# Attention block with cached keys: the second turn's keys transposed on TensorE, idle products at the start, other first loads, new orders

## The chip, the core and the metric

One core of a Trainium2 chip runs the whole program. Its engines are TensorE (PE: matmuls and transposes into PSUM), VectorE (DVE), ScalarE (ACT), GpSimd (POOL, here only the identity matrix) and SyncE (SP, here the queue that issues every load and store to the 16 DMA engines). The metric is the device time of one execution in microseconds; lower is better. Where runs are compared, it is the median.

## The reference

```
x: 8 x 112 x 640    k_cache, v_cache: 8 x 32 x 512 x 192    wq: 640 x 6144    wo: 6144 x 640   (bf16)
q      = (x @ wq) as 8 x 32 heads x 112 x 192
scores = einsum("bhqd,bhkd->bhqk", q, k_cache) * 192 ** -0.5
p      = softmax(scores)
o      = einsum("bhqk,bhkd->bhqd", p, v_cache)
out    = o as 8 x 112 x 6144 @ wo
```

## The kernel before, in words

**Turns and steps.** A turn t is one batch element with one half of the heads (16 heads): t = 0 to 15, batch t mod 8, half t div 8. A step n works on four heads: n = 0 to 63, turn n div 4. A unit u (0 to 15) is one head's keys or values within its turn, 512 rows of 192.

**Orders written out by hand.** Four texts at the top of the file (SP_WORK, PE_WORK, ACT_WORK, DVE_WORK) are lists of words, one list for each engine, and each engine works strictly in the order of its list. A word is a letter with numbers. Class Plan keeps for each operation what it depends on, and who must have read a buffer or a PSUM bank before it is overwritten (function `take` does this for the eight banks), and turns both into semaphore waits. An engine whose next word has to wait holds up all words behind it.

On SP: X loads token chunks of x (chunks of 128 tokens, 160 KB each), W loads a piece of wq for heads in pairs (W0.2.2: half 0, from pair 2, two pairs, 960 KB; one pair is 480 KB), U loads keys as they stand (untransposed) of the first turn into `kn`, K3 loads the keys of turn 3 transposed by the DMA engines into `kt[3 % 2]`, V10.8 loads the values of turn 10, units 8 to 15 (1536 KB), Y1.0 loads one half of wo's rows of head half 1 (1920 KB), Z stores. `kn` lies in the place of wo (`wo_flat`), and so does `vx`, the third home of values, used once by V1.0; Y0.0 and V1.0 therefore wait until the first turn's keys have been transposed. K of turn t waits for the last scores of turn t - 2, as there are two key buffers; a V waits until the products of the values that lay in its place are done.

On PE: X5.7 transposes token chunk 5 with bank 7; A0.3.6 and B0.3.4 compute the queries of head pair 3 for two batch elements (A: two 128-row blocks, ten matmuls of 224 columns; B: one, five matmuls); K6.0 transposes unit 6 of the first turn's keys, six 128 x 128 transposes; S5 computes the scores of step 5 into banks 0 to 3; T5.0.4 and T5.1.5 transpose its probabilities (eight transposes each) and V5.4 multiplies them with the values (16 + 16 matmuls); O are groups of four matmuls with wo, G and L the like of the last two turns, F the final transposes of the output.

On ACT and DVE: x, k, a, b, t, v copy the results of X, K, A, B, T, V out of PSUM (a and b are "q copies"); m is the scaling of the scores with the row minimum of the negated values, e the exponential with its row sum, r the reciprocal, n the normalisation, c two copies of queries into `qh` for step n (the "q copy" ahead of a step's scores), p, g, l the sums of O, G and L.

**Where the profile's lines are.** L399 X loads, L404 U loads, L411 W, L419 Y, L432 K, L445 V, L453 stores; L468 X, L477 K, L490 A and B, L521 to L538 scores, L548 T, L568 and L581 V, L597 O, L612 G, L627 L, L638 F; L650 all copies (function `copy`; the tile it writes tells which: kt, xT_sb, acc_q for queries, pT_sb, oT_sb), L675 and L676 c, L685 m, L695 e, L703 r, L710 n, L735 and L737 p.

**The start.** Before its first scores PE transposes x, fills queries, and transposes the first turn's keys, which come untransposed by U0.4, U4.8 and U8.16 (768, 768 and 1536 KB); all later turns' keys come transposed by DMA (K1 to K15). The two loads that are issued together in the profile at 23.79 are K1 and K2; K2 waits for the scores of step 3.

Q_PLACES gives each head pair's queries a place in `qp` for each pair of turns.

## Time and profile before

| | us |
|---|---|
| time, median of 3 runs (459.57 to 460.03) | 459.64 |
| the profiled execution's own time | 460.54 |
| its span, first to last instruction | 458.7 |
| PE busy | 438.4 |
| DVE busy | 360.8 |
| ACT busy | 347.3 |

The span is what the profile's times count in, from the first instruction; the execution's own time has some 1.8 us around it. A row of a view of instructions has start, duration, engine, line, operation, written tile <- read tiles, shapes, and in brackets the idle time of the engine before it and what ended it. A row of the chain of waits has start, share of the path, engine and line; matmuls there are counted from one end to the next, so many of them give the price of one in a dense row. A row of a view of windows has the stretch, its length, the busy time (and number of instructions) of PE, PEld, DVE, ACT and POOL, the granted PE clock, DMA's share and GB/s. A row of instruction groups has busy time, mean duration in ns, and idle time before.

### The profile page before, as it was taken

The numbers are of one execution on the slowest core, as the hardware profiler recorded it, in microseconds if no ns is written. First come the engines' busy times: TensorE is split into PE (matmuls) and PEld (weight loads), VectorE is DVE, ScalarE is ACT, GpSimd is POOL, SyncE is SP. The second block draws the span as 40 slices with busy tenths as digits, with TensorE's granted clock in tenths as the row PEclk, the third lists the DMA queues.
The fourth block names the chain that finished last, engine by engine and source line by source line (L and its number), as shares of the span: only waits on it lengthen the run. The fifth ranks groups of instructions, "written<-read, shape, count | busy, mean of one in ns | idle before, by whom it ended". The sixth has DMA issues, their size and how long they took to land.

```text
span 458.7 us, 14942 instructions
## 1 busy us (share of the span) xinstructions
PE 438.4 (96%) x6307; PEld 399.2 (87%) x6307; DVE 360.8 (79%) x1165; ACT 347.3 (76%) x787; POOL 0.7 (0%) x6
## 2 busy tenths in 40 slices
PE   4999899999999999999999999997999999999996
PEld 3889789888999888998989899997998999899996
DVE  0566768878889986789898888886868988979781
ACT  2577879867877878687886789766787788777683
POOL 0000000000000000000000000000000000000000
PEclk9899999999999999999999999999999999999999
DMA  8999999999989999999999999999999999996501
GB/s 278 372 350 224 241 327 352 237 306 287 260 215 247 362 275 214 308 243 331 206 337 209 309 235 326 300 189 368 225 274 260 281 287 261 219 253 222 178 14 51
DMA packets 234321, 119.63 MB, mean 261 GB/s; under 512 B 185744, under 2 KB 234256, under 8 KB 234256
## 3 DMA queue, kind: packets, MB, share of 16 engines
q1 hardware_dynamic: 234256, 118.69, 106.5%
q8 instruction: 49, 0.80, 0.7%
q14 instruction: 16, 0.13, 0.1%
HBM read 70.35 MB, written 1.15 MB: 156 GB/s over the span
## 4 chain that ended last, share of the span: by engine, by line
PE 87%; ACT 4%; DMA 4%; DVE 3%; issue 1%; SPq 0%; ACTq 0%
PE ps L490 18%; PE ps L597 17%; PE ps L581 12%; PE ps L548 10%; PE ps L536 7%; PE ps L568 7%; PE ps L521 6%; PE ps L523 6%; DMA wq_sb<-in_wq_dram 2%; ACT p_sb L695 2%; DMA vt<-in_v_cache_dram 2%; PE ps L612 1%; DVE s_sb L685 1%; PE ps L627 1%; ACT acc_q L650 1%
## 5 line engine op out<-in xcount | busy, mean ns | idle before, releaser
L695 ACT ACTIVATE p_sb<-s_sb,nmx 112x512 bf16<-112x512 f32 x256 | 183.1, 717 | 42.3 <-DVE s_sb L685 40.7
L685 DVE TENSOR_SCALAR_CACHE_REDUCE s_sb<-ps 112x512 f32<-112x512 f32 x256 | 172.9, 684 | 41.3 <-PE ps L538 16.9
L490 PE MATMUL ps<-xT_sb,wq_sb 128*128 128x224 bf16 x960 | 110.0, 262 | 2.7 <-DMA wq_sb<-in_wq_dram 0.9
L597 PE MATMUL ps<-oT_sb,wo_sb 128*128 128x224 bf16 x840 | 95.0, 259 | 0.8 <-ACT acc_q L650 0.4
L490 PEld LDWEIGHTS ps<-xT_sb,wq_sb 128*128 128x128 bf16 x960 | 88.6, 99 | 7.4 <-DMA wq_sb<-in_wq_dram 1.9
L710 DVE TENSOR_SCALAR p_sb<-p_sb,rinv 112x512 bf16<-112x512 bf16 x256 | 84.6, 349 | 3.2
L597 PEld LDWEIGHTS ps<-oT_sb,wo_sb 128*128 128x128 bf16 x840 | 77.1, 98 | 2.5 <-issue 0.7
L650 ACT ACTIVATE acc_q<-ps 128x224 bf16<-128x224 f32 (+1 forms) x128 | 55.9, 447 | 24.6 <-PE ps L490 19.8
L650 ACT ACTIVATE pT_sb<-ps 128x896 bf16<-128x896 bf16 x64 | 58.3, 911 | 13.0 <-PE ps L548 12.8
L548 PE MATMUL ps<-ident,p_sb 112*128 112x112 bf16 x1024 | 65.3, 213 | 0.1
L650 ACT ACTIVATE oT_sb<-ps 128x672 bf16<-128x672 f32 x64 | 46.5, 727 | 18.5 <-PE ps L581 16.2
L548 PEld LDWEIGHTS ps<-ident,p_sb 112*128 112x128 bf16 x1024 | 57.7, 98 | 2.5 <-DVE p_sb L710 0.7
L581 PE MATMUL ps<-pT_sb,vt 128*128 128x112 bf16 x992 | 59.5, 213 | 0.0
L581 PEld LDWEIGHTS ps<-pT_sb,vt 128*128 128x128 bf16 x992 | 49.8, 98 | 4.9
L695 ACT ACTIVATION_READ_ACCUMULATOR p_sb<-s_sb,nmx 112x1 f32 x256 | 49.2, 192 | 0.0
L650 DVE COPY pT_sb<-ps 128x896 bf16<-128x896 bf16 x64 | 39.7, 620 | 12.0 <-PE ps L548 11.2
L568 PEld LDWEIGHTS ps<-pT_sb,vt 128*64 128x64 bf16 x992 | 27.3, 109 | 16.8 <-ACT p_sb L695 7.2
L568 PE MATMUL ps<-pT_sb,vt 128*64 128x112 bf16 x992 | 36.2, 215 | 5.4 <-DVE p_sb L710 2.6
L521 PE MATMUL ps<-kt,acc_q 128*112 128x256 bf16 x128 | 35.2, 275 | 1.3 <-DVE kt L650 0.7
L523 PE MATMUL ps<-kt,acc_q 128*112 128x256 bf16 x128 | 34.9, 273 | 0.0
L521 PE MATMUL ps<-kt,qh 128*112 128x256 bf16 x128 | 34.9, 272 | 0.0
L523 PE MATMUL ps<-kt,qh 128*112 128x256 bf16 x128 | 34.9, 272 | 0.0
(50 smaller groups left out, 453.2 us busy)
## 6 DMA issues: line engine op xcount, KB each, us to landing
vt<-in_v_cache_dram SPq DMA_DIRECT2D x31, 1536.0 KB, 9.1
wo_sb<-in_wo_dram SPq DMA_DIRECT2D x4, 1920.0 KB, 13.5
wq_sb<-in_wq_dram SPq DMA_DIRECT2D x7, 960.0 KB, 10.7
wo_sb<-in_k_cache_dram SPq DMA_DIRECT2D x2, 768.0 KB, 9.1
wo_sb<-in_k_cache_dram SPq DMA_DIRECT2D x1, 1536.0 KB, 14.2
wo_sb<-in_v_cache_dram SPq DMA_DIRECT2D x1, 1536.0 KB, 7.8
out_dram<-xT_sb SPq DMA_DIRECT2D x8, 140.0 KB, 3.3
wq_sb<-in_wq_dram SPq DMA_DIRECT2D x2, 480.0 KB, 6.4
```

Source lines behind the costliest of these rows:

```text
L490: mm = e.matmul(ps[:, bank, j * S2:(j + 1) * S2], wq_sb[:, dc, c0:c0 + 128], xT_sb[:, dc, bp * S2:(bp + 1) * S2], start=(dc == 0), stop=(d ...
L521: e.matmul(ps[0:SQ, 2 * j, hs], ev, ktb[:, :, 0, cs(i)], start=(h == 0), stop=False, skip_group_check=True)
L523: mm = e.matmul(ps[0:SQ, 2 * j + 1, hs], od, ktb[:, :, 2, cs(i)], start=(h == 0), stop=False, skip_group_check=True)
L536: m1 = e.matmul(ps[0:SQ, 2 * j, hs], ev, ktb[0:64, :, 1, cs(i)], start=False, stop=True, skip_group_check=True)
L548: mm = e.transpose(psb[:, bank, c:c + SQ], p_sb[:, (4 * n + 2 * j + h) % 8, q * 128:(q + 1) * 128], ident[0:SQ, 0:SQ])
L568: mm = e.matmul(ps[64 * h:64 * h + 64, b0 + j, SQ:2 * SQ], vtb[:, h0 + 2 * j + h, d0:d0 + 64], pT(j, h, q), start=(q == 0), stop=(q == 3))
L581: mm = e.matmul(ps[:, b0 + j, 2 * h * SQ:(2 * h + 1) * SQ], vtb[:, h0 + 2 * j + h, d0:d0 + 128], pT(j, h, q), start=(q == 0), stop=(q == 3))
L597: mm = e.matmul(ps[:, bank, j * S2:(j + 1) * S2], wo_sb[:, KU * (u % 2) + k, m * 128:(m + 1) * 128], oT_sb[:, u % NO, k, :], start=(k == 0 ...
L650: return e.activation(dst, src, ACTF.Copy) if eng == "ACT" else e.tensor_copy(dst, src)
L685: return e.tensor_scalar(s_sb[:, a, :].rearrange("p (e c) -> p e c", e=2), ps[0:SQ, 2 * j:2 * j + 2, h * 256:(h + 1) * 256], -scale, None, ...
L695: return e.activation(p_sb[:, k, :], s_sb[:, a, :], ACTF.Exp, bias=nmx[:, k:k + 1], scale=-1.0, accum_out=rsum[:, k:k + 1])
L710: return e.tensor_scalar(p_sb[:, k, :], p_sb[:, k, :], rinv[:, k:k + 1], None, op0=ALU.mult)
```

## The change

Five things change together.

1. U words carry a turn: U1.0.8 and U1.8.16 load the second turn's keys untransposed into the same `kn`, after the first turn's unit in that place has been transposed (`load_kn`), and K1 leaves SP's list. PE's list has 16 more K words (K1.3.4: turn 1, unit 3, bank 4), ACT's and DVE's lists 8 more copies each, into `kt[1]`. The scores of turn 1 wait for these copies. K3, which overwrites `kt[1]`, and K2, which overwrites `kt[0]`, wait for the copies too; Y0.0 and V1.0 wait for both turns' transposes.
2. D words: products of the identity with itself into a bank that nobody reads (`idle_products`). PE's list begins with 8 and 20 of them.
3. The first loads stand in another order on SP: W0.1.1 ahead of the first keys, then U0.0.4 and U0.4.8 one behind the other. V0.8 stands behind U1.8.16.
4. Q_PLACES has other places, and the lists of all engines are in a new order throughout. They hold the same work apart from 1 and 2. On SP, Y1.0 moves ahead of K10, Y0.1 ahead of K3, and V4.0 behind K5.
5. A further word, P, and functions for it (probabilities transposed by DMA) are new in the code; SP's list holds no such word, so the list `by_dma` is empty and they do nothing.

```
 SP_WORK = """
-X0.0.2 W0.0.1 U0.4 W0.1.1 W0.2.2 X1.2.4 X2.4.7 U4.8 W0.6.2 W0.4.2 U8.16 V0.0 V0.8
-K1
-K2 V1.0 V1.8 Y0.0 V2.0
-K3 V2.8 Y0.1 V3.0
-K4 V3.8 V4.0
-K5 V4.8 W1.4.2 W1.2.2 V5.0 W1.0.2
-K6 V5.8 V6.0
-K7 V6.8 W1.6.2 V7.0
-K9 V8.8 V9.0
-K10 V9.8 Y1.0 V10.0
-K15 V14.8 V15.0 V15.8 Z1 Z2 Z0 Z5 Z3 Z4 Z6 Z7
+X0.0.2 W0.0.1 W0.1.1 U0.0.4 U0.4.8 W0.2.2 X1.2.4 W0.6.2 W0.4.2 U0.8.16 X2.4.7 V0.0 U1.0.8 U1.8.16 V0.8
+K2 V1.0 V1.8 Y0.0 V2.0 Y0.1
+K3 V2.8 V3.0
+K4 V3.8
+K5 V4.0 V4.8 W1.0.2 W1.4.2 W1.2.2 V5.0
+K6 V5.8 W1.6.2 V6.0
+K7 V6.8 V7.0
+K9 V8.8 V9.0 Y1.0
+K10 V9.8 V10.0
+K15 V14.8 V15.0 V15.8 Z0 Z5 Z1 Z4 Z3 Z2 Z6 Z7
...
 PE_WORK = """
-X1.4 X0.6 A0.0.6 B0.0.4 K0.6 B0.1.5 A0.1.7 K2.3 K3.0 K1.2 A0.3.6 X2.5
-S0 A0.2.7 K6.0 B0.3.4 K5.5 X4.0 X3.1 X5.7 B0.7.6 B0.2.5 K7.2 K4.0 B0.6.7
-S1 B1.2.7 B1.3.6 B1.6.7 A0.6.6 K11.0 K8.1 A0.7.7 T0.0.4 K12.1 B0.5.6 X6.0 A0.4.7 K9.0 K15.3 A0.5.6 K10.5 B0.4.7 K13.4
-A1.6.6 B1.0.7 T0.1.5
-S2 V0.4 K14.6 A1.1.7 A1.0.6 B1.7.7 T1.0.4 T1.1.5
-S3 V1.4 A3.0.7 T2.0.4 T2.1.5 B1.1.6 A1.4.7 B3.7.6
-S4 V2.4 B2.4.7
-S5 A2.4.6 B2.5.7 T3.0.4 A1.2.6 T3.1.5 A1.3.7
...
+D1.8.3 D0.20.3 X1.0 X0.4 A0.0.6 B0.1.5 A0.1.6 B0.0.4 K0.2.1 K0.0.0 K0.3.3 K0.1.2 K0.5.4 K0.4.5
+S0 B0.2.5 A0.3.7 A0.2.6 B0.3.5 K0.7.1 K0.6.4 A0.7.6 X3.5 B0.7.7
+S1 B0.6.6 B0.4.7 X2.4 A0.4.6 A0.5.7 K0.13.5 K0.12.0 K0.11.3 B0.5.7 K0.10.1 T0.0.4 K0.9.3 B1.0.6 X5.7 K0.14.0 K0.15.4
+K0.8.1 T0.1.5 A0.6.7
+S2 V0.4 A1.4.6 X6.1 B1.1.7 A1.1.6 T1.0.4
+S3 T1.1.5 K1.3.4 A3.0.7 K1.7.1 A1.6.6 V1.4 K1.4.0 K1.6.1 K1.1.2 K1.9.0 T2.0.4 K1.12.1 K1.5.6 K1.2.7 T2.1.5 X4.3
+K1.15.2 K1.0.1 A1.0.6 K1.14.7 K1.13.4
+S4 V2.4 K1.10.7 K1.8.0 A2.0.6 B1.7.7 K1.11.5 A3.5.6
+S5 B1.6.6 T3.0.4 B3.4.6 A1.3.7 T3.1.5 B1.4.6
...
 ACT_WORK = """
...
-e3.0 b1.1 e3.1 t2.0 e3.2 e3.3
-e4.0 a1.4 b3.7 e4.1 e4.2 v2 b2.4 e4.3 a2.4
...
+e3.0 k1.3 e3.1 k1.7 a3.0 a1.6 v1 e3.2 k1.1 k1.5 t2.0 k1.9 k1.15 e3.3 k1.13 a1.0
+e4.0 e4.1 v2 a2.0 b1.7 e4.2 k1.11 a3.5 e4.3 b1.6
...
 DVE_WORK = """
...
-m3.0 c4 c5 r2.1 n2.2 n2.3 m3.1 t2.1 m3.2 m3.3 r3.0
-m4.0 n3.0 m4.1 n3.1 m4.2 m4.3 r3.1 n3.2 n3.3 r4.0 n4.0
...
+m3.0 m3.1 t1.1 m3.2 m3.3 r2.1 n2.2 c4 k1.4 k1.6 n2.3 k1.12 k1.2 t2.1 k1.0 x4 r3.0 n3.0 n3.1 k1.14 r3.1
+m4.0 m4.1 c5 n3.2 k1.10 n3.3 m4.2 k1.8 m4.3 r4.0 c6 n4.0
...
 
         v_units = [(t, lo) for t in range(NT) for lo in (0, 8)]
         v_home = [0, 1, 2] + [(i + 1) % 2 for i in range(3, len(v_units))]
-        x_piece, wq_piece, kn_piece = {}, {}, {}
+        x_piece, wq_piece, kn_piece, by_dma = {}, {}, {}, []
         for kind, *a in work["SP"]:
+            if kind == "P":
+                by_dma.append(a[0])
             if kind == "X":
                 x_piece.update({c: ("X", a[0]) for c in range(a[1], a[2])})
             elif kind == "W":
                 wq_piece.update({(a[0], a[1] + i): ("WQ", *a) for i in range(a[2])})
             elif kind == "U":
-                kn_piece.update({u: ("KN", *a) for u in range(*a)})
+                kn_piece.update({(a[0], u): ("KN", *a) for u in range(a[1], a[2])})
+        kn_turns = sorted({t for t, _ in kn_piece})
 
         def q_both(m, lp):
             return [("Qa", m, lp), ("Qb", m, lp)]
...
                 return e.dma_start(xn[c0 // 4][:, c0 % 4:c0 % 4 + c1 - c0, :], src.rearrange("(c p) d -> p c d", p=128))
             add("SP", ("X", j), [], emit, f"mX{j}", 16)
 
-        def load_kn(lo, hi):
-            def emit(e):
-                return e.dma_start(kn[:, lo:hi, :], k_cache[0, lo:hi].rearrange("u (r q) d -> r u (q d)", q=4))
-            add("SP", ("KN", lo, hi), [], emit, f"mKN{lo}", 16)
+        def load_kn(t, lo, hi):
+            def emit(e):
+                return e.dma_start(kn[:, lo:hi, :], k_cache[t, lo:hi].rearrange("u (r q) d -> r u (q d)", q=4))
+            old = [("KT", t - 1, u) for u in range(lo, hi)] if t else []
+            add("SP", ("KN", t, lo, hi), old, emit, f"mKN{t}_{lo}", 16)
 
         def load_wq(half, lp, n):
             def emit(e):
...
             if half:
                 old = [d for w in range(u, NM, 2) for d in o_parts(w)]
             else:
-                old = [("KT", i) for i in range(HU)] + ([("PVm", 4, 1), ("PVm", 5, 1)] if u else [])
+                old = [("KT", *i) for i in kn_piece] + ([("PVm", 4, 1), ("PVm", 5, 1)] if u else [])
             add("SP", ("WO", half, u), old, emit, f"mWO{u}", 16)
 
         def load_k(t):
...
                 src = k_cache[b, half * HU:(half + 1) * HU].rearrange("u (r q) d -> (u r) (q d)", q=4)
                 return e.dma_start_transpose(kt[t % 2][:].rearrange("p a m c -> p (a m) c"), src)
             old = [("St", step_of(t - 2, s), 3) for s in range(4)] if t > 1 else []
+            old += [("evK", t - 2, u) for u in range(HU)] if t - 2 in kn_turns else []
             add("SP", ("K", t), old, emit, f"mK{t % 2}", 16)
 
         def v_tile(i):
...
                 return e.dma_start(v_tile(i)[:], src)
             old = [j for j in range(i) if v_home[j] == v_home[i]][-1:]
             old = [("PVm", step_of(v_units[j][0], v_units[j][1] // 4 + s), 1) for j in old for s in range(2)]
-            old += [("KT", u) for u in range(HU)] if v_home[i] == 2 else []
+            old += [("KT", *i) for i in kn_piece] if v_home[i] == 2 else []
             add("SP", ("V", t, lo), old, emit, f"mV{v_home[i]}", 16)
 
         def store(b):
             def emit(e):
                 return e.dma_start(out[b], xT_sb[0:SQ, b % DC, 0:D])
             add("SP", ("OUT", b), [("oout", b)], emit, f"mOUT{b % DC}", 16)
+
...
 
         holder = {}
...
             add("PE", ("XT", c), [x_piece[c]], emit)
             take(("XT", c), bank, ("XT", c), [("evX", c)])
 
-        def k_transposes(u, bank):
+        def k_transposes(t, u, bank):
             def emit(e):
                 for c in range(6):
                     mm = e.transpose(psb[:, bank, c * 128:(c + 1) * 128], kn[:, u, c * 128:(c + 1) * 128], ident[:, :])
                 return mm
-            add("PE", ("KT", u), [kn_piece[u]], emit)
-            take(("KT", u), bank, ("KT", u), [("evK", u)])
+            add("PE", ("KT", t, u), [kn_piece[t, u]], emit)
+            take(("KT", t, u), bank, ("KT", t, u), [("evK", t, u)])
+
+        def idle_products(i, n, bank):
+            def emit(e):
+                for _ in range(n):
+                    mm = e.matmul(ps[:, bank, 0:128], ident[:, :], ident[:, :], start=True, stop=True)
+                return mm
+            add("PE", ("D", i), [], emit)
+            take(("D", i), bank, ("D", i), [])
 
         def q_fill(part, m, lp, bank):
             half, bp = divmod(m, B // 2)
...
                         mm = e.matmul(ps[0:SQ, 2 * j + 1, hs], od, ktb[:, :, 2, cs(i)], start=(h == 0), stop=False,
                                       skip_group_check=True)
                     return mm
-                add("PE", ("Sm", n, j), [("qc", n)] + ([("evK", 4 * s + i) for i in range(4)] if t == 0 else [("K", t)]),
+                add("PE", ("Sm", n, j), [("qc", n)] + ([("evK", t, 4 * s + i) for i in range(4)] if t in kn_turns else [("K", t)]),
                     emit)
                 for b in (2 * j, 2 * j + 1):
                     take(("Sm", n, j), b, ("Sm", n, j), [("smax", n, 2 * j), ("smax", n, 2 * j + 1)])
...
             copy(eng, ("evX", c), [("XT", c)], xT_sb[:, :, c * 128:(c + 1) * 128],
                  psb[:, bank_of["XT", c], 0:D].rearrange("p (c s) -> p c s", c=DC))
 
-        def ev_k(eng, u):
-            copy(eng, ("evK", u), [("KT", u)], kt[0][:].rearrange("p a m c -> p (a m) c")[:, :, u * 128:(u + 1) * 128],
-                 psb[:, bank_of["KT", u], 0:768].rearrange("p (c r) -> p c r", c=6))
+        def ev_k(eng, t, u):
+            copy(eng, ("evK", t, u), [("KT", t, u)], kt[t][:].rearrange("p a m c -> p (a m) c")[:, :, u * 128:(u + 1) * 128],
+                 psb[:, bank_of["KT", t, u], 0:768].rearrange("p (c r) -> p c r", c=6))
 
         def ev_q(eng, part, m, lp):
             blocks = (0, 1) if part == "a" else (2,)
...
             def emit(e):
                 return e.activation(p_sb[:, k, :], s_sb[:, a, :], ACTF.Exp, bias=nmx[:, k:k + 1], scale=-1.0,
                                     accum_out=rsum[:, k:k + 1])
-            add(eng, ("exp", n, i), [("smax", n, i)] + ([("PT", n - 2, i // 2)] if n > 1 else []), emit)
+            old = [] if n < 2 else [("P", n - 2)] if n - 2 in by_dma else [("PT", n - 2, i // 2)]
+            add(eng, ("exp", n, i), [("smax", n, i)] + old, emit)
 
         def rc(eng, n, j):
             k = (4 * n + 2 * j) % 8
...
                  xT_sb[0:SQ, b % DC, 0:D], psb[0:SQ, bank_of["OF", b], 0:D])
 
         bank_of = {(k + "T", *a[:-1]): a[-1] for k, *a in work["PE"] if k in "XK"}
-        loads = {"X": load_x, "W": load_wq, "U": load_kn, "V": load_v, "K": load_k, "Y": load_wo, "Z": store}
+        loads = {"X": load_x, "W": load_wq, "U": load_kn, "V": load_v, "K": load_k, "Y": load_wo, "Z": store,
+                 "P": p_transposes}
         for kind, *a in work["SP"]:
             loads[kind](*a)
-        on_pe = {"X": x_transposes, "K": k_transposes, "A": lambda *a: q_fill("a", *a), "B": lambda *a: q_fill("b", *a),
+        on_pe = {"D": idle_products, "X": x_transposes, "K": k_transposes, "A": lambda *a: q_fill("a", *a), "B": lambda *a: q_fill("b", *a),
                  "S": scores, "T": transposes, "V": values, "O": o_sums, "G": o_six, "L": o_last, "F": o_final}
         for kind, *a in work["PE"]:
             on_pe[kind](*a)
```

The rows of the lists that are left out, and Q_PLACES, are changed in order only.

More of the change, by code (lines that the diff above doesn't have):

```diff
@@ L160 @@
[L160 to L172 removed]
+x1 a0.0 b0.1 b0.0 a0.1 k0.1 k0.5
@@ L454, in store, with p_spare, p_transposes @@
             add("SP", ("OUT", b), [("oout", b)], emit, f"mOUT{b % DC}", 16)
+        def p_spare(n):
+            return wq_flat[:, by_dma.index(n) * 16 * SQ:(by_dma.index(n) + 1) * 16 * SQ].rearrange("p (c s) -> p c s", c=16)
+        def p_transposes(n):
+            k = 4 * n % 8
+            def emit(e):
+                return e.dma_start_transpose(p_spare(n), p_sb[:, k:k + 4, :].rearrange("p a c -> p (a c)"))
+            old = [d for m in range(NM // 2, NM) for lp in range(LP) for d in q_both(m, lp)]
+            add("SP", ("P", n), [("norm", n, i) for i in range(4)] + old, emit, f"mP{n % 2}", 16)
         holder = {}
@@ L713, in ev_pt @@
         def ev_pt(eng, n, j):
-            copy(eng, ("evPT", n, j), [("PT", n, j)] + ([("PVm", n - 1, j)] if n else []),
+            old = [("PVm", w, j) for w in range(n) if w not in by_dma][-1:]
+            copy(eng, ("evPT", n, j), [("PT", n, j)] + old,
                  pT_sb[:, j, :, :].rearrange("p h c -> p (h c)"), psb[:, bank_of["PT", n, j], 0:8 * SQ])
```

378 lines of the change are left out of this document (190 added, 188 removed), and 16 rows, old and new, of the table Q_PLACES.

## The prediction

> **What bounds the kernel now.** The page first: the share of each engine.
>
> ```profile
> span 458.7 us, 14942 instructions
> PE 438.4 (96%) x6307; PEld 399.2 (87%) x6307; DVE 360.8 (79%) x1165; ACT 347.3 (76%) x787; POOL 0.7 (0%) x6
> ```
>
> PE is the bound: it is busy for 438.4 of 458.7 us. So time can be won in two ways only: less work on PE, or less waiting of PE. The view of windows, cut at the first scores (16.35) and at the second turn's first scores (51.73), says where it waits.
>
> ```profile
> 0.00:16.35 16.35, 9.82 (x79) 8.36 (x80) 2.79 (x7) 4.80 (x8) 0.70 (x6) 0.90 0.91 305
> 16.35:51.73 35.38, 33.74 (x438) 30.38 (x436) 24.08 (x72) 26.70 (x62) 0.00 (x0) 1.00 1.18 287
> 51.73:454.80 403.07, 394.70 (x5795) 360.49 (x5793) 333.97 (x1087) 314.88 (x717) 0.00 (x0) 1.00 1.08 258
> ```
>
> Of the 20.3 us that PE is idle, 6.5 lie before the first scores, 1.6 between them and turn 1, 8.4 in the long rest, and 3.9 after PE's end, where the last window is cut. The share before the last figure of a row is DMA's: it is about 1 everywhere, so loads are a second, near bound.
>
> PE's timeline and the chain of waits give the start, and the price of each kind of work.
>
> ```profile
> 4.03 1.23 PE L468 MATMUL ps<-ident,oT_sb 128*128 128x128 bf16 x10 [4.03 <-DMA oT_sb<-in_x_dram]
> ...
> 9.60 0.51 PE L477 MATMUL ps<-ident,wo_sb 128*128 128x128 bf16 x6 [0.96 <-DMA wo_sb<-in_k_cache_dram]
> 11.02 2.36 PE L490 MATMUL ps<-xT_sb,wq_sb 128*128 128x224 bf16 x15 [0.91 <-DMA wq_sb<-in_wq_dram]
> ...
> 16.35 0.27 PE L521 MATMUL ps<-kt,acc_q 128*112 128x256 bf16 x1
> ...
> 17.89 1.13 PE L490 MATMUL ps<-xT_sb,wq_sb 128*128 128x224 bf16 x10
> ```
>
> ```profile
> 13.38 1.90 PE ps L477 x18
> ...
> 30.16 0.96 PE ps L490 x10
> ...
> 33.83 0.67 PE ps L477 x12
> ...
> 39.89 0.51 PE ps L568 x16
> 40.41 0.89 PE ps L581 x16
> ...
> 44.03 0.79 PE ps L548 x16
> ...
> 51.73 0.11 PE ps L521
> ```
>
> Until 11 us PE's long waits end with loads. Prices, from these rows: an A fill of ten matmuls (L490) 0.96, a B of five 0.48, a K group of six transposes 0.34 (0.67/2), an X group of five 0.28, one step's scores 1.54 (16.35 to 17.89), a T group 0.40, a V group 1.40 (0.51 + 0.89).
>
> **The added PE work.** Turn 1's 16 units cost 96 transposes at 0.056 us (0.67/12): **+5.4 us**, all on the bounding engine. The 28 idle products stand ahead of the first data. At the unwarmed price of a 128-column product (1.90/18 = 0.106) they take 3.0 us; PE waits until 4.03 today, and they end near 4.6 if they start at 1.6 (an estimate: POOL writes the identity first, with six instructions of 0.7 us in all). The half microsecond is hidden, since the next thing after them that counts is a load at 11 us. Without that cover it would cost 0.5.
>
> What the products do to PE's clock is judged by these windows, whose third figure from the right is the granted clock.
>
> ```profile
> 4.90:8.30 3.40, 2.77 (x18) 2.02 (x16) 0.49 (x1) 0.92 (x2) 0.00 (x0) 1.00 0.99 321
> 8.30:11.70 3.40, 1.53 (x17) 1.11 (x15) 0.56 (x1) 0.55 (x2) 0.00 (x0) 1.00 1.06 382
> 11.80:15.10 3.30, 3.30 (x28) 2.98 (x27) 1.00 (x3) 0.81 (x2) 0.00 (x0) 0.50 1.07 370
> ```
>
> A stretch busy for 1.53 of 3.40 us was followed by one at clock 0.50; a stretch busy for 2.77 was not. The products should raise the clock early, but that wins nothing while loads set the pace, and the gaps that follow can lose it again; I count zero, with +1.7 (half of 3.4 us at half speed) as the upper end. The Trainium skill, page TensorE: Matmul & The Clock Gate, Part 4: PE-mode transpose, states that transposes do not count as busy for this clock. By that rule the added transposes would tend to the unwarmed price, 96 x 0.106 = 10.2 us. The trace disagrees: the last stretch above ends in 18 transposes, and 12 transposes at 33.83 ran at 0.056.
>
> **The first loads.** Landing times come from the DMA issues and their time to landing (10.5 us belongs to the issue at 7.51, 14.2 to that at 13.23).
>
> ```profile
> 7.51 1.76 SPq L404 DMA_DIRECT2D wo_sb<-in_k_cache_dram  x1
> ...
> 13.23 2.20 SPq L404 DMA_DIRECT2D wo_sb<-in_k_cache_dram  x1
> ...
> 23.79 35.28 SPq L432 DMA_TRANSPOSE kt<-in_k_cache_dram  x2
> ```
>
> ```profile
> DMA to landing us min/median/max: 10.5/10.5/10.5
> ```
>
> ```profile
> wo_sb<-in_k_cache_dram SPq DMA_DIRECT2D x1, 1536.0 KB, 14.2
> ```
>
> Units 4 to 7 landed at 18.0 and 8 to 15 at 27.4; between them came 960 + 960 + 1536 KB, so 368 KB/us. The first four pieces (320, 480, 768, 480 KB) are the same four in another order, so all of them are in by 11.0 again. The new list then has units 4 to 7 next: 11.0 + 768/368 = 13.1 us, and two K groups of them stand ahead of step 0's scores: 13.8. The chain on DVE is longer: three of its copies of K groups and the two halves of the q copy come between the last transposes and the scores.
>
> ```profile
> L650 ACT ACTIVATE kt<-ps 128x768 bf16<-128x768 bf16 x7 | 5.7, 811 | 2.0 <-PE ps L477 2.0
> L650 DVE COPY kt<-ps 128x768 bf16<-128x768 bf16 x9 | 5.0, 553 | 11.3 <-PE ps L477 11.2
> L675 DVE COPY qh<-acc_q 64x672 bf16<-64x672 bf16 x7 | 2.3, 329 | 0.9 <-ACT acc_q L650 0.6
> ```
>
> The third of four K groups ends near 12.1 (11.0 + 3 x 0.34), and the first copy starts: 12.1 + 3 x 0.55 + 2 x 0.33 = 14.4, so scores at 14.5 instead of 16.35. The new list has 0.6 less work ahead of them (one X and one A fewer, two K more: -0.28 - 0.96 + 0.67), so the wait recovered is 1.9 - 0.6 = **-1.3 us** (bounds 0, if the clock or a load is late, and -2.3).
>
> **From the first scores to turn 1.** The old list holds 4 X, 10 A, 13 B, 12 K, 4 scores, 6 T and 2 V here: 32.4 us by the prices, and 35.4 passed, so 3.0 were lost. In the new list the weights follow at 368 KB/us from 13.1 on: W0.2.2 at 15.7, W0.6.2 at 19.2, W0.4.2 at 21.8, units 8 to 15 at 26.0, and by the prices their users come at 16.0, 19.6, 23.3 and 26.0. So PE should run nearly without waits: I take **-2.2**, bounds -3.0 and 0. Turn 1's copies lie here too.
>
> ```profile
> L695 ACT ACTIVATE p_sb<-s_sb,nmx 112x512 bf16<-112x512 f32 x256 | 183.1, 717 | 42.3 <-DVE s_sb L685 40.7
> L650 ACT ACTIVATE pT_sb<-ps 128x896 bf16<-128x896 bf16 x64 | 58.3, 911 | 13.0 <-PE ps L548 12.8
> L650 ACT ACTIVATE oT_sb<-ps 128x672 bf16<-128x672 f32 x64 | 46.5, 727 | 18.5 <-PE ps L581 16.2
> ```
>
> ```profile
> L650 ACT ACTIVATE acc_q<-ps 128x448 bf16<-128x448 f32 x14 | 7.4, 539 | 4.9 <-PE ps L490 4.9
> ```
>
> Between the scores of steps 3 and 4 ACT's new list has 4 exps, 7 K copies, 3 q copies, one V and one T copy: 2.87 + 5.68 + 1.62 + 0.73 + 0.91 = 11.8 us. PE's has one step of scores, 13 K, 3 A, 3 T, one V and one X: 1.5 + 4.4 + 2.9 + 1.2 + 1.4 + 0.3 = 11.7. That is the tightest spot; the other nine copies go to DVE and to the steps around it.
>
> New waits on SP: the second key loads wait for turn 0's transposes (the last, K0.8, at about 30), and V0.8, K2 and all later loads queue behind them. V0.8's user is V2.4, behind step 4's scores at 50; after 26.0 come 480 KB and four pieces of 1536 KB, so V0.8 lands near 44. V1.0 and Y0.0 now wait for K1.11, behind step 4's scores, at some 54; before, SP sat in the issue of K1 and K2 until 59.1 (23.79 + 35.28). So neither costs time. The transposing load that goes frees DMA, and here nobody waits for it.
>
> **The long rest.** Two places lose much.
>
> ```profile
> 50.00:60.00 10.00, 8.85 (x111) 7.40 (x109) 7.86 (x27) 8.29 (x21) 0.00 (x0) 1.00 1.24 282
> ```
>
> ```profile
> 312.16 0.62 DVE L650 COPY pT_sb<-ps 128x896 bf16<-128x896 bf16 x1
> 313.43 0.27 PE L538 MATMUL ps<-kt,acc_q 64*112 64x256 bf16 x1
> 316.30 0.58 PE L568 MATMUL ps<-pT_sb,vt 128*64 128x112 bf16 x16 [2.60 <-DVE p_sb L710]
> ```
>
> ```profile
> 277.35 0.58 SPq L419 DMA_DIRECT2D wo_sb<-in_wo_dram  x1
> 282.75 24.27 SPq L432 DMA_TRANSPOSE kt<-in_k_cache_dram  x1
> 307.07 0.58 SPq L445 DMA_DIRECT2D vt<-in_v_cache_dram  x1
> ```
>
> ```profile
> DMA to landing us min/median/max: 9.1/9.1/9.1
> ```
>
> At 313 PE waits for V10.8, whatever the row names: its copies were done at 312.8, and V10.8, issued at 307.07 behind K11, landed 9.1 later, at 316.2. Ahead of K11 stood Y1.0 (277.35), 1920 KB or 5.2 us. The new list issues Y1.0 one turn earlier, ahead of K10, so K11 and V10.8 come sooner and K10 and V9.8 later: **-2.0** (bounds -2.7, and 0 where the wait only moves). The 1.15 us at 50 to 60 follow ten q copies in ACT's rows of steps 4 and 5; the new rows hold nine and a K copy: **-0.5** (0 to -1.15). The rest, some 4 to 5 us of PE's idling, is small waits that the new orders deal anew. Work between a step's scores and its first T group is at least 8.5 us in the new list (last step apart), in the old 7.6, 8.2 and 8.3 at three steps, and the end has one more L group between V63 and the last sums: **-1.0**, bounds +2.5 and -2.5.
>
> **Sum.** +5.4 - 1.3 - 2.2 - 2.0 - 0.5 - 1.0 = **-1.6 us**: span 457.1 for 458.7. The profiled execution took 460.54 in all, 1.84 around its span and 0.9 over the median of the runs, 459.64; the change against that median gives **458.0 us**, 0.35% faster.
>
> **Rivals.** (1) *The copies bind, slower.* ACT's 11.8 us beside 11.7 of PE between scores 3 and 4 hold up PSUM banks, and the terms -2.2, -0.5 and -1.0 go: 5.4 - 1.3 - 2.0 = +2.1, **461.7**. It decides once PE waits there for over 2 us on ACT or DVE copies of keys. For: the sums; against: DVE was busy for 24.1 and ACT for 26.7 of 35.4 us before. (2) *The V wait only moves* to K10 or V9.8 behind Y1.0: the -2.0 goes, **460.0**, and a new wait of a microsecond makes it 461. For: DMA is at 1 all along. (3) *The clock falls again* in the gaps near 12 to 14.5: +1.7, **459.7**. The Trainium skill, same page, Part 1: The HAM clock gate, has one idle window of about 3.4 us as the condition; the trace shows the fall after a window that was 45% busy. (4) *The new orders remove most small waits*: -2.2, -2.0 and -1.0 reach their lower bounds of -3.0, -2.7 and -2.5, another -3.0, **455.0**. For: 8.4 us are there to win. Against: every order leaves some.
>
> **Chances.** Forecast 0.34, rival 1 0.24, 2 0.14, 3 0.08, 4 0.20. Within 0.2% (0.9 us, what a measurement of this kernel can tell) lie 0.05 of the forecast, 0.07 of rival 2 and 0.03 of 3: 0.15. Faster is the rest of the forecast and rival 4: 0.49; slower rival 1 and the rests of 2 and 3: 0.36. The forecast's own range is 456.5 to 459; the range for all is 453.5 to 463.0: rival 1 with the clock's 1.7 (463.4) and rival 4 with -2.3 at the start and -1.15 at 50 to 60 (453.4) lie at its ends.
>
> **What would show it.** First scores near 14.5 and turn 1's near 50; no wait of over 1 us at V10.8; a K group at 0.34 us for turn 1. Wrong if first scores stay near 16, if PE waits on key copies in steps 3 to 5, or if a K or V load after Y1.0 is late.

## The result, and the profile after

The changed kernel takes **452.41 us** (median of 4 runs, 451.3 to 453.81) beside 459.61 for the kernel before (4 runs, 457.88 to 460.03): ratio 0.9852, 95% interval 0.9814 to 0.989. The profiled execution took 452.13 us with a span of 450.2. The forecast was 458.0, its range 453.5 to 463.0: the direction was right, the size far too small, and the time lies outside the range.

The first lines of the page of after:

```profile
span 450.2 us, 15210 instructions
...
PE 441.7 (98%) x6431; PEld 405.9 (90%) x6431; DVE 364.0 (81%) x1173; ACT 350.1 (78%) x795; POOL 0.7 (0%) x6
```

PE is busy 3.3 us longer than before (438.4) and the span is 8.5 us shorter, so PE's idle time fell from 20.3 to 8.5 us. Where it fell is read from the view of windows of after, cut again at the first scores (14.48) and at turn 1's first scores (49.90); the columns are window, length, and the busy time of PE, PEld, DVE, ACT and POOL, then granted clock, DMA share and GB/s.

```profile
0.00:14.48 14.48, 10.18 (x104) 8.94 (x104) 2.75 (x8) 5.49 (x9) 0.70 (x6) 1.00 0.87 297
14.48:49.90 35.42, 35.17 (x489) 32.96 (x490) 26.88 (x79) 30.00 (x67) 0.00 (x0) 1.00 1.12 328
49.90:446.90 397.00, 396.39 (x5841) 364.02 (x5838) 334.39 (x1088) 313.90 (x721) 0.00 (x0) 1.00 1.08 261
```

Idle of PE: 4.3 us before the first scores (6.5 before the change), 0.3 from there to turn 1 (1.6), and **0.6 in the long rest, where it was 8.4**. The view of waits of after, for PE, names nearly all that is left; its columns are the waiting line, what it waited for, microseconds in total, times, the longest.

```profile
PE ps L504 <- POOL ident L861: 1.5, 1, 1.5
PE ps L517 <- DMA wq_sb<-in_wq_dram: 1.0, 1, 1.0
PE ps L517 <- DVE xT_sb L678: 0.6, 1, 0.6
PE ps L496 <- DMA wo_sb<-in_k_cache_dram: 0.6, 1, 0.6
PE ps L548 <- DVE qh L704: 0.5, 1, 0.5
PE ps L666 <- DVE acc_q L793: 0.2, 1, 0.2
PE ps L517 <- ACT acc_q L678: 0.2, 1, 0.2
```

The first five lie ahead of the first scores. Behind them two waits of 0.2 us are left in 435 us. Neither the 2.6 us at V10.8 nor any wait of a V, T or O word on a copy is in the list.

The time from turn 1's first scores to the end is 458.73 - 51.57 = 407.16 before and 450.20 - 49.90 = 400.30 after. The new list holds 3.4 us more work there (three K groups, 1.0, and five B fills, 2.4, that stood ahead of step 4 before). So it takes 6.9 us less for 3.4 us more work: by the prices, 10.3 us less are lost. The view of windows shows 7.8 of it as idle, and 0.6 lies behind PE's end (3.9 us before, 3.3 after); the other 1.9 lie in stretches that it counts as busy. The forecast had 3.5 for these 10.3 (9.5 in the means of three profiles each, in the table below). That difference of 6.8 us is nearly the whole miss (the span fell by 8.5, forecast 1.6), and the experiments ask where it comes from: from the written orders, or from the loads, which the direct load of turn 1's keys relieves.

### The profile page after: what moved, and what is told of

It is laid out like the page before. It is cut to its first block, busy times and chain, and to the rows that moved or that the text cites. A ratio compares the mean times of both kernels' runs of the same rounds, so it can differ in the third digit from the quotient of the medians.

```text
span 450.2 us, 15210 instructions
## 1 busy us (share of the span) xinstructions
PE 441.7 (98%) x6431; PEld 405.9 (90%) x6431; DVE 364.0 (81%) x1173; ACT 350.1 (78%) x795; POOL 0.7 (0%) x6
## 4 chain that ended last, share of the span: by engine, by line
PE 95%; DMA 2%; ACT 2%; DVE 1%; issue 0%; SPq 0%
PE ps L517 20%; PE ps L625 18%; PE ps L609 13%; PE ps L575 11%; PE ps L563 8%; PE ps L595 7%; PE ps L548 6%; PE ps L550 6%; PE ps L496 2%; DMA wq_sb<-in_wq_dram 2%; PE ps L655 1%; PE ps L640 1%; PE ps L666 0%; ACT acc_q L678 0%; DVE kt L678 0%; ACT oT_sb L678 0%
## 5 line engine op out<-in xcount | busy, mean ns | idle before, releaser
L723 ACT ACTIVATE p_sb<-s_sb,nmx 112x512 bf16<-112x512 f32 x256 | 183.1, 718 | 35.2 <-DVE s_sb L713 33.8
L517 PE MATMUL ps<-xT_sb,wq_sb 128*128 128x224 bf16 x960 | 107.3, 260 | 1.9 <-DMA wq_sb<-in_wq_dram 1.0
L625 PE MATMUL ps<-oT_sb,wo_sb 128*128 128x224 bf16 x840 | 93.3, 259 | 0.0
L678 ACT ACTIVATE pT_sb<-ps 128x896 bf16<-128x896 bf16 x64 | 58.4, 913 | 15.9 <-PE ps L575 13.9
L678 ACT ACTIVATE oT_sb<-ps 128x672 bf16<-128x672 f32 x64 | 46.4, 726 | 22.6 <-PE ps L609 20.3
L548 PE MATMUL ps<-kt,acc_q 128*112 128x256 bf16 x128 | 35.2, 275 | 0.5 <-DVE qh L704 0.5
```

The costliest lines, as they stand in the source:

```text
L517: mm = e.matmul(ps[:, bank, j * S2:(j + 1) * S2], wq_sb[:, dc, c0:c0 + 128], xT_sb[:, dc, bp * S2:(bp + 1) * S2], start=(dc == 0), stop=(d ...
L548: e.matmul(ps[0:SQ, 2 * j, hs], ev, ktb[:, :, 0, cs(i)], start=(h == 0), stop=False, skip_group_check=True)
L625: mm = e.matmul(ps[:, bank, j * S2:(j + 1) * S2], wo_sb[:, KU * (u % 2) + k, m * 128:(m + 1) * 128], oT_sb[:, u % NO, k, :], start=(k == 0 ...
L678: return e.activation(dst, src, ACTF.Copy) if eng == "ACT" else e.tensor_copy(dst, src)
L723: return e.activation(p_sb[:, k, :], s_sb[:, a, :], ACTF.Exp, bias=nmx[:, k:k + 1], scale=-1.0, accum_out=rsum[:, k:k + 1])
```

## The experiments

For comparison across kernels, the text uses the stretch from 50 to 440 us, where every kernel here does plain steady work, and PE's idle time in it: 390 us less PE's busy time in the view of windows.

**1. No idle products.**

```diff
-D1.8.3 D0.20.3 X1.0 X0.4 A0.0.6 ...
+X1.0 X0.4 A0.0.6 ...
```

> The changed kernel without the 28 idle products. As the prediction had it (loads set the pace until 13 us, products worth nothing): first scores at 14.5, span within 0.5 us of the changed kernel's 450.2. Rival, the clock: without the products PE starts slow, a stretch near 8 to 15 us falls to clock 0.50, and the first scores or the fills behind them come 1 to 2 us later, with the end of the span as much later.

Measured: 453.28 us (10 runs), ratio to before 0.9905, interval 0.9869 to 0.9941; span 451.8, first scores at 15.50. The interval overlaps that of after. PE's waits in its view:

```profile
PE ps L487 <- DMA oT_sb<-in_x_dram: 3.9, 1, 3.9
PE ps L548 <- DVE qh L704: 1.3, 1, 1.3
```

The 1.5 us that PE waits in after before the products, and the products themselves, become a wait of 3.9 for the first tokens. The idle time from 50 to 440 is 1.0 us, so the clean rest doesn't hang on the products. The span is 1.6 us longer, where the expectation allowed 0.5, and the start shows why: the twenty query matmuls that follow W0.1.1 took nearly twice as long as in after. PE's timeline, without the products and with them:

```profile
8.39 3.83 PE L517 MATMUL ps<-xT_sb,wq_sb 128*128 128x224 bf16 x20 [0.59 <-DMA wq_sb<-in_wq_dram]
```

```profile
8.93 2.09 PE L517 MATMUL ps<-xT_sb,wq_sb 128*128 128x224 bf16 x20 [1.05 <-DMA wq_sb<-in_wq_dram]
```

So W0.1.1 came 0.5 us earlier, and the first scores 1.0 us later. The rival's slow start did come, though the granted clock of the windows reads 1.00 all along. What the products are worth in time isn't settled: the medians differ by 0.9 us, and the intervals overlap.

**2. Turn 1's keys by the transposing load, all else as changed.**

```diff
-... W0.4.2 U0.8.16 X2.4.7 V0.0 U1.0.8 U1.8.16 V0.8
+... W0.4.2 U0.8.16 X2.4.7 V0.0 K1 V0.8
-K1.3.4 ... K1.11.5   (16 words on PE, 16 copies on ACT and DVE)
```

> The changed kernel with the second turn's keys loaded transposed by DMA again, ahead of V0.8; all else as changed. Theory A (the new orders as such have fewer waits, and the keys' way has no part in the 6.9 us that the prediction missed): 5.4 us less PE work; K1 lands near 46 and V0.8 near 50, step 4's scores want them at 45.5 and V2 at 47.5, so 3 to 4 us of waiting near 46 to 51; from 60 us on PE waits for under 1 us in all; span 448 to 449. Theory B (the transposing load that went relieves the loads for the rest of the run): waits on V and K loads come back after 60 us, over 3 us in all, span 451 or more.

Measured: 455.64 us (10 runs), ratio 0.9947, interval 0.9922 to 0.9972; span 453.6, 3.4 more than after, though PE has 96 transposes (5.4 us) less to do. The view of waits, PE:

```profile
PE ps L595 <- DMA vt<-in_v_cache_dram: 4.0, 3, 2.5
...
PE ps L595 <- DMA wo_sb<-in_v_cache_dram: 0.9, 1, 0.9
...
PE ps L548 <- DMA kt<-in_k_cache_dram: 0.6, 1, 0.6
```

V0.8 is late at 48 us (the 2.5), V1.0 at 67 (the 0.9), K3 at 101 (the 0.6), V2.8 at 107; behind 110 us no wait is over 0.5 us. These waits sum to 5.3 us. They cost more than their length: right behind the longest, PE ran at half its clock for 3.41 us, some 1.7 us lost (the section on the hardware has the rows). So the direct load pays: its 5.4 us of transposes buy off the waits for loads at 40 to 110 us and that slow stretch. The span is what theory B expected, but the waits end at 110 us: the direct load doesn't explain the clean rest behind that, which this kernel has too.

**3 and 4. Y1.0 in its old place in the new lists, and in its new place in the old lists.**

```diff
 # 3, in the changed kernel
-K9 V8.8 V9.0 Y1.0
-K10 V9.8 V10.0
+K9 V8.8 V9.0
+K10 V9.8 Y1.0 V10.0
 # 4, in the kernel before
-K9 V8.8 V9.0
-K10 V9.8 Y1.0 V10.0
+K9 V8.8 V9.0 Y1.0
+K10 V9.8 V10.0
```

> The changed kernel with Y1.0 back behind V9.8 on SP, nothing else. Theory A with the prediction's step for V10.8: PE waits 2 to 2.9 us at V10.8 again (near 307), span 452 to 453. Theory B (loads have slack since K1 went): no wait over 0.5 us there, span 450 to 450.5.

> The kernel before with Y1.0 moved ahead of K10 on SP, nothing else. The prediction's step: the wait of 2.7 us at V10.8 goes, span 2.0 to 2.7 us shorter than 458.7. Its rival 2: the wait moves to K10 or V9.8, span the same within 0.7 us.

Measured: 3 takes 452.36 us (4 runs), ratio 0.9878, interval 0.9827 to 0.993, span 449.5, idle from 50 to 440 0.3 us as in after: V10.8 lands 2.7 us ahead of its use. 4 takes 461.34 us (10 runs), ratio 1.0074, interval 1.0043 to 1.0106: slower than before. The view of waits of 4 has the V wait still, at V9.8 (it ends at 288.45) instead of V10.8:

```profile
PE ps L568 <- DMA vt<-in_v_cache_dram: 3.6, 1, 3.6
```

Behind this wait, too, PE ran at half its clock for 3.41 us. So the step that the forecast valued at -2.0 wins nothing in the new lists and costs in the old ones: rival 2's mechanism, in the lists it was drawn from, with a slow stretch on top. What the forecast took for Y1.0's doing has another cause.

**5. Old lists up to step 18, new ones behind** (turn 1's keys by the transposing load, no products). **6. New lists up to step 4, old ones behind** (turn 1's keys by the direct load).

```diff
 # 5: SP has the lines of before to K4, those of after from K5; PE, ACT, DVE change lists at S18, e18.0, m18.0
-S18 O2.0.0.7 O2.0.1.7 O2.1.0.6 O2.0.2.7 ... T16.1.5 ... V16.4 ...
+S18 O2.0.0.7 O2.0.1.7 O2.0.2.7 B3.1.6 V16.4 B3.6.6 T17.0.4 T17.1.5
 # 6: SP has the lines of after to V0.8, those of before from K2; PE, ACT, DVE change lists at S4, e4.0, m4.0
-S4 V2.4 B2.4.7
+S4 V2.4 K1.10.7 K1.8.0 B1.6.6 B1.7.7 K1.11.5 B1.3.6 B3.7.7 B1.2.6 B2.4.7
```

> The lists of before up to the scores of step 18 (first loads, turn 1's keys by the transposing load, no idle products), the changed kernel's lists from there on; the places of the later q tiles are dealt anew, since the two kernels' places don't join. Theory O (the long rest is won by the written orders themselves): step 18 starts near 145 as before, and from there on the waits of before, some 9 us in this stretch, fall to the changed kernel's 2 to 3: span near 452. Theory L (the rest is won because turn 1's keys come by a direct load, which gives every later load a lead): no lead here, so V10.8 is waited for again and the span stays at 456 to 459.

> The changed kernel's lists up to the scores of step 4 (first loads, idle products, turn 1's keys by a direct load and on TensorE; the last three K groups and five B fills just behind), the lists of before from there on. First scores at 14.5 and step 4 near 50 under both theories. Theory O: the waits of before come back, with 2.7 at V10.8 and some 5 in small ones: 49.9 + (458.7 - 51.6) + 2.4 for the five B fills + 1.0 for the three K groups = a span near 460.5. Theory L: the loads have their lead, V10.8 is not waited for and the small waits go: near 452 to 454.

Measured: 5 takes 455.42 us (4 runs), ratio 0.9932, interval 0.9907 to 0.9958, span 455.2: neither theory's figure. V10.8 is in time (it lands 3.2 us ahead of its use) and the copies' waits from step 18 on are mostly gone, but one wait of 2.5 us stands at V5.8, whatever releaser the row names (K6 landed at 182.5, just as it was needed, and V5.8, issued behind it, landed at 186.60, 0.1 us before the row starts). PE's timeline:

```profile
186.73 0.58 PE L591 MATMUL ps<-pT_sb,vt 128*64 128x112 bf16 x16 [2.52 <-DVE p_sb L735]
```

6 takes **457.92 us** (10 runs), ratio 0.9984, interval 0.9961 to 1.0007: no change from before that can be measured, with the whole new start and turn 1's keys on TensorE, and only the later orders old. Its span of 456.0 lies between theory O's 460.5 and theory L's 452 to 454.

**7 and 8. Before and after once more, unchanged.**

> The kernel before once more, unchanged. Theory O: the waits for copies come back at the same places with the same length (0.5 at 92.5, 0.62 at 107.4, 0.61 at 159.5, 0.80 at 173.2), whatever the loads do; waits for loads (0.9 at 261.6 for V8.8, 2.7 at V10.8, 0.44 at V11.8) may differ by a microsecond or two, since the lists fix only when a load is issued. If the copies' waits move as well, they are no matter of the lists.

> The changed kernel once more, unchanged. Its loads had leads of 1.8 us and more in the long rest, so a shift of a microsecond or two does not reach TensorE: idle of TensorE in the long rest again under 2 us, span 449.5 to 451. If a wait for a load of over 1 us shows up here, the clean rest of the first profile was luck of the loads.

PE's timeline of before once more (start, length, engine, line, and in brackets the idle time ahead and its releaser):

```profile
51.77 0.29 PE L521 MATMUL ps<-kt,acc_q 128*112 128x256 bf16 x1 [1.68 <-DMA kt<-in_k_cache_dram]
...
160.21 1.71 PE L597 MATMUL ps<-oT_sb,wo_sb 128*128 128x224 bf16 x16 [0.45 <-ACT acc_q L650]
...
174.14 0.58 PE L568 MATMUL ps<-pT_sb,vt 128*64 128x112 bf16 x16 [0.64 <-ACT p_sb L695]
...
315.17 0.58 PE L568 MATMUL ps<-pT_sb,vt 128*64 128x112 bf16 x16 [1.01 <-DMA vt<-in_v_cache_dram]
```

Two kinds of wait part here. The copies' waits come back: the V group of step 20 starts at 174.14 in both profiles, with the same 0.64 us of idle ahead of it. The loads' waits move: V10.8 cost 2.60 us in the first profile and 1.01 in this one. And first scores at 14.53, 1.8 us earlier than in the first profile, win nothing: K1 lands late and turn 1 starts at 51.77, as before at 51.57.

After once more took 454.36 us (span 452.4). Its rest has one load wait:

```profile
288.19 0.58 PE L595 MATMUL ps<-pT_sb,vt 128*64 128x112 bf16 x16 [0.81 <-DMA vt<-in_v_cache_dram]
```

That is V9.8, behind Y1.0 and K10: under the 1 us that the expectation drew as its line. The idle from 50 to 440 is 1.1 us. The span is above the 449.5 to 451 that was expected, since its first scores came at 15.98 instead of 14.48.

**9. Six words moved in the old lists**, each at a place where PE waits for a copy.

```diff
-S20 V18.4 O3.1.0.7 B3.1.6 O2.3.0.6 O3.1.1.7 ...
+S20 V18.4 B3.1.6 O3.1.0.7 O3.1.1.7 O2.3.0.6 ...
-e11.0 ... v9 b3.0 e11.2 t10.0 e11.3
+e11.0 ... v9 t10.0 b3.0 e11.2 e11.3
-m9.0 ... n9.1 c11 r9.1 p0.2
+m9.0 ... n9.1 p0.2 c11 r9.1
-m21.0 r20.0 m21.1 n20.0 t19.1 ...
+m21.0 r20.0 m21.1 t19.1 n20.0 ...
-m22.0 ... n21.1 r21.1 n21.2 n21.3 t20.1 ...
+m22.0 ... n21.1 t20.1 r21.1 n21.2 n21.3 ...
-m32.0 n31.1 m32.1 t30.1 ...
+m32.0 n31.1 t30.1 m32.1 ...
```

> The kernel before with six single words moved, each at a place where the trace of before shows PE waiting for a copy that stands late in its own list: B3.1 two places ahead of O2.3.0 on the same bank (0.61 us at 159.5), t10.0 ahead of b3.0 (0.62 at 107.4), p0.2 ahead of c11 (0.50 at 92.5), t19.1 ahead of n20.0 (0.28 at 165.5), t20.1 ahead of n21.2 (0.80 at 173.2), t30.1 ahead of m32.1 (0.45 at 238.0): 3.26 us in all. Theory O (each wait is the price of its place in the lists, and goes through to the end): these six places are free of waits and the span is near 455.5. Theory T (the loads take it back): the loads of before have leads of 0.1 to 2 us (V8.8, V10.8, V11.8 0.1, K8 0.5, V7.8 0.7), so a faster TensorE only waits longer for them: the six places are free, the load waits grow by about the same, and the span stays within 457.5 to 459.

Measured: 457.92 us (10 runs), ratio 0.998, interval 0.9948 to 1.0011; span 456.4, between the two theories' figures. Idle from 50 to 440 is 5.4 us. At B3.1, t10.0, t19.1 and t20.1 the waits are gone. At the other two the next thing is late instead, in PE's timeline:

```profile
94.51 0.58 PE L568 MATMUL ps<-pT_sb,vt 128*64 128x112 bf16 x16 [0.56 <-issue]
...
240.39 0.96 PE L548 MATMUL ps<-ident,p_sb 112*128 112x112 bf16 x16 [0.27 <-ACT oT_sb L650]
```

With p0.2 moved up, V8 waits at 94.5 for the T copy that stands behind; with t30.1 moved up, a T group waits at 240.4. The waits for loads didn't grow as theory T had it: behind step 4's first scores PE's timeline has 2.6 us of them here, 3.7 and 3.4 in the first two profiles of before. From step 4 to the end the profile took 404.5 us, where three of before took 406.3 to 407.2; in the medians of the runs no gain can be measured.

**10 and 11. Half of turn 1's keys by a transposing load.** In 11 V1.0 stands ahead of K2 as well.

```diff
-... V0.0 U1.0.8 U1.8.16 V0.8
-K2 V1.0 V1.8 Y0.0 V2.0 Y0.1
+... V0.0 U1.0.8 V0.8 H1.8.16        # H: units 8 to 15 of turn 1, transposed by the DMA
+K2 V1.0 V1.8 Y0.0 V2.0 Y0.1         # 10
+V1.0 K2 V1.8 Y0.0 V2.0 Y0.1         # 11
-K1.9.0 K1.12.1 K1.15.2 K1.14.7 K1.13.4 K1.10.7 K1.8.0 K1.11.5   (and their copies)
```

> The changed kernel with only units 0 to 7 of turn 1's keys transposed on TensorE; units 8 to 15 come by one transposing load of half the size, issued behind V0.8. 48 transposes fewer: -2.7 us on TensorE. In the run with all of turn 1's keys by the transposing load the loads of 40 to 110 us lost 7.5 to 9.6 us of lead. If the loss goes with the transposed bytes, half of it, 4 to 5, is about what the leads of the changed kernel hold there (V0.8 6.9, V1.0 4.3, K3 3.0, V2.8 3.8, V4.0 2.1): waits of about 1 us, span near 448.5. If any transposing load in this stretch puts the loads behind, as it did whole, the saving is given back: 450 to 453.

> The kernel with half of turn 1's keys by a transposing load, with V1.0 issued ahead of K2 instead of behind it. There V1.0 was issued at 57.4, when K2's issue let SP go, landed at 65.0 and PE waited 0.94 us for it; K2 landed 14.7 us ahead of its use. With V1.0 first it is issued once K1.7 is transposed, near 47, and that wait goes: span near 449.2 for 450.1. If the wait only moves to another load of 90 to 150 us (K3 and V4.0 had leads of 0.1), 450.

Measured: 10 takes 452.73 us (4 runs), ratio 0.9885, interval 0.9845 to 0.9926, span 450.1, as after. Turn 1's steps run 2.6 us ahead of after's, and that is given back piece by piece, first at V1.0 (PE's timeline):

```profile
65.10 0.58 PE L604 MATMUL ps<-pT_sb,wo_sb 128*64 128x112 bf16 x16 [0.78 <-DMA wo_sb<-in_v_cache_dram]
```

11 takes 454.42 us (4 runs), ratio 0.9893, interval 0.9834 to 0.9953, span 452.8. V1.0 is in time, and Y0.0 and K3 are late in its place (PE's timeline):

```profile
78.69 0.54 PE L634 MATMUL ps<-oT_sb,wo_sb 128*128 128x224 bf16 x4 [2.27 <-DMA wo_sb<-in_wo_dram]
101.97 0.29 PE L557 MATMUL ps<-kt,acc_q 128*112 128x256 bf16 x1 [1.52 <-DMA kt<-in_k_cache_dram]
```

So from 40 to 110 us PE's work and the loads are in balance in the changed kernel: 2.7 us taken off PE come back as waits. No version tried beats after.

**12 to 15. The mixed kernel (6) twice more, before and after a third time.**

> The kernel with the changed start and the lists of before from step 4 on, once more. Its first profile had 1.2 us of waits for loads behind step 4 (V11.8, V13.8) where three profiles with the old start had 3.2 to 4.1. If that is the direct load's doing (theory L in part), this one shows 0.5 to 2 again, and step 4 to the end takes 406 to 407.5. If it was that execution alone (theory O whole), 3 to 4 us come back and step 4 to the end takes about 409.5.

> The same kernel a third time, with the same expectations: 406 to 407.5 from step 4 to the end, or about 409.5.

> The kernel before a third time. Theory L in part: waits for loads of 3 to 5 us behind step 4 again, 406.3 to 408 from step 4 to the end. Theory O whole: anything from 1 to 5 us.

> The changed kernel a third time. Both theories: waits for loads behind step 4 of 0 to 1 us, 400 to 401.2 from step 4 to the end.

Single times: 459.39 and 457.42 for the mixed kernel, 458.86 for before, 452.8 for after. One row of the view of windows for each, the third profile of before, of the mixed kernel and of after:

```profile
50.00:440.00 390.00, 382.34 (x5538) 348.26 (x5536) 328.00 (x1068) 307.16 (x702) 0.00 (x0) 1.00 1.13 267
```

```profile
50.00:440.00 390.00, 385.98 (x5607) 352.85 (x5605) 330.05 (x1073) 309.06 (x709) 0.00 (x0) 1.00 1.09 264
```

```profile
50.00:440.00 390.00, 389.68 (x5710) 357.85 (x5708) 333.23 (x1087) 311.91 (x718) 0.00 (x0) 1.00 1.09 264
```

PE's idle time in this stretch, in all three profiles of each:

| kernel | idle of PE from 50 to 440 us | mean | step 4 to the end |
|---|---|---|---|
| before | 8.2, 9.2, 7.7 | 8.3 | 407.2, 406.5, 406.3 |
| mixed: new to step 4, old behind | 5.1, 5.7, 4.0 | 5.0 | 406.7, 407.3, 405.3 (with 3.4 more work) |
| after | 0.3, 1.1, 0.3 | 0.6 | 400.3, 401.0, 400.2 (with 3.4 more work) |

The third profile of the mixed kernel has no wait for a load behind step 4 at all: its 4.0 us are what the old orders cost in copies' waits. This PE timeline of it shows the two waits quoted from before, of the same length:

```profile
162.04 1.71 PE L620 MATMUL ps<-oT_sb,wo_sb 128*128 128x224 bf16 x16 [0.45 <-ACT acc_q L673]
...
175.98 0.24 PE L590 MATMUL ps<-pT_sb,vt 128*64 128x112 bf16 x2 [0.64 <-ACT p_sb L718]
```

Before has some 4 us more, and nearly all of that is waits for loads (0.4 to 1.7 of it, in two profiles, is the wait for K1 at the stretch's start). In three profiles of before and three of the mixed kernel, whose lists are the same from step 8 on, SP sat longer in the issue of K11 with the old start (24.3, 24.5 and 24.4 us; mixed 21.6, 23.2 and 21.0), and V10.8, issued right behind it, was waited for in all three of before and in none of the mixed. SP's timeline of the third profile of each, K11's issue and V10.8's:

```profile
281.42 24.43 SPq L432 DMA_TRANSPOSE kt<-in_k_cache_dram  x1
305.89 0.58 SPq L445 DMA_DIRECT2D vt<-in_v_cache_dram  x1
```

```profile
283.57 21.04 SPq L434 DMA_TRANSPOSE kt<-in_k_cache_dram  x1
304.65 0.59 SPq L448 DMA_DIRECT2D vt<-in_v_cache_dram  x1
```

So both theories hold in part. Of the 7.7 us of idle that the stretch lost, 8.3 - 5.0 = 3.3 go with the changed start and 5.0 - 0.6 = 4.4 with the orders behind step 4. By the time from step 4 to the end, in means, it is 0.2 + 3.4 = 3.6 for the start and 5.9 for the orders. This split holds for the start changed first. The new lists do without the direct load as well: experiment 2, which lacks it, has no long wait for a load behind 110 us.

Theory L's lead carried forward is borne out in part, at about a microsecond. K6, the load of turn 6's keys, landed 1.0, 0.0 and 0.0 us ahead of its use in the three profiles of before, and 1.8, 1.7 and 1.4 in those of the mixed kernel; V8.8 landed just as it was waited for in all three of before, and 2.2, 0.8 and 2.8 us ahead in the mixed kernel. What makes the transposing loads of turns 10 and 11 take SP less time in the mixed kernel stays open, and so does what the new order of the loads does and what the new lists of PE, ACT and DVE do: experiment 6 takes both back at once.

## Why the prediction missed, point by point

- **Work on PE, +5.4.** Right. In after a K group of turn 1 takes 0.34 us (two groups in 0.67), and with half of turn 1's transposes gone (experiment 10) steps 3 to 5 took 15.9 us instead of 18.2, 2.3 less where 48 x 0.056 = 2.7 were taken off. The row is from the chain of waits of after (start, length, engine, line):

```profile
49.39 0.67 PE ps L496 x12
```

- **Start, -1.3.** First scores came at 14.48, forecast 14.5. But as a gain of the change it was mis-sized, and that it fits the first pair of profiles is luck: the profile of before on which it rests had a stretch at clock 0.50 ahead of its first scores, and two more profiles had them at 14.53 and 14.96. After had 14.48, 15.98 and 13.81. In means that is 0.5 us, no more than the 0.6 of work that the new list has less there. The products, counted as zero because loads set the pace, do change the pace of PE's first fills (experiment 1).
- **To turn 1, -2.2.** Turn 1's scores came at 49.90, forecast "near 50". By the prices the stretch ahead of them lost 2.8 us before (35.2 passed, 32.4 of work) and 0.4 after (35.4 and 35.0): right in size. A second limit was not named, though: K1's landing. In the profile that the forecast rests on, K1 landed at 50.4, only 1.1 us before PE came to it at 51.57. With first scores 1.8 us earlier, before still started turn 1 at 51.77, behind a 1.68 us wait for K1. The sentence "the transposing load that goes frees DMA, and here nobody waits for it" holds for K1 by that one microsecond alone, and was wrong for the loads behind it up to 110 us (experiment 2).
- **50 to 60 us, -0.5.** The two waits of before there (on ACT's q copies and on the step's scores) are gone in all three profiles of after. More than forecast, in the right place.
- **V10.8, -2.0.** The wait went, and the reason given was wrong. Y1.0 back in its old place brings no wait (experiment 3); Y1.0 moved in the old lists costs 0.7% (experiment 4). The wait goes with the changed start (the mixed kernel) and with the new orders on the old start (experiment 5, where Y1.0 is early too), and it isn't a fixed 2.7 us either: 2.6, 1.0 and 2.3 us of idle in three profiles.
- **Small waits, -1.0. This is the step that failed**, together with the -2.0: "small waits that the new orders deal anew", with bounds of 2.5 to either side. It took them to be much the same in any order. They are a property of this one order, place by place, 4.0 us in the stretch from 50 to 440 without a load's wait (mixed kernel, third profile), and the new orders leave 0.3. Some 4 us more were waits for loads, of which the forecast saw only the one at V10.8. The terms for the long rest were -3.5 in all; it gave 10.3.
- **Rivals.** The nearest was the fourth (455.0), with a chance of 0.20, held down by "every order leaves some". After leaves 0.3 to 1.1 us in 390. Rival 1, copies of keys binding, didn't come: PE's waits behind the first scores hold none on them. Rival 2 came where the lists are old (experiment 4), and as one wait of 0.8 us in after's second profile. Rival 3, the clock, came in one of after's three profiles and cost some 1.2 us at the first scores (next section but one); it came in before as well, so it is no cost of the change.
- **Range.** Its lower end was built from bounds on the start, the way to turn 1, the V wait and 50 to 60 us, with 2.5 us for all small waits of a span that lost 8.4 in them and in loads. The bound should have been the idle time itself.

## What to carry to other kernels

Where orders are written by hand, split the bounding engine's idle time into waits for copies and waits for loads, and profile twice: waits for copies that return to the hundredth of a microsecond are the price of this list, and a new list can win all of them, so their whole sum is the bound. Waits for loads move between executions; an early gain ahead of a load that lands no earlier is no gain, and a load moved in the queue moved the wait in two of three trials here (experiments 4 and 11; not 3). Mending six such places word by word left new waits at two of them (experiment 9), because the next copy in the same list was late right behind.
